# The second expert's first product by seven products of quarters, with the sums of x and of its weights made during the first expert

## The chip, the cores and the metric

One core of a Trainium2 chip runs the whole program. TensorE (PE) multiplies, VectorE (DVE), ScalarE (ACT) and GpSimd (POOL) work on tiles in SBUF and PSUM, and SyncE (SP) issues most DMAs. The metric is the device time of one execution in microseconds, the median of several runs; lower is better.

## The reference

A causal attention with a forgetting bias (2 batches, 8 heads, 576 positions, head size 64) gives 1152 tokens of 512 numbers. A layer of 8 experts and a bilinear layer follow, all in float32:

```python
logits = x @ w_gate; P = np.exp(logits - logits.max())
for _ in range(8):
    P /= P.sum(1, keepdims=True) + 1e-09
    P /= P.sum(0, keepdims=True) + 1e-09
    P *= N / E
for e in range(E):
    h = np.maximum(x @ w1[e], 0.0)      # 1152 x 1024
    out += P[:, e:e + 1] * (h @ w2[e])
...
return (x2 @ w_a) * (x2 @ w_b) @ w_out
```

Every expert sees all tokens.

## The kernel before

Each float32 operand is held as two float16 parts, high and low, and each product is three matmuls (high by high, high by low, low by high). `x` stands transposed in `xt`, two parts of four chunks of 128 rows by 1152 tokens, written tile by tile (9 tiles of 128 tokens) as the attention ends. The first expert (number 0) has plain products per tile, put in between the attention's work as filling for PE.

An expert's first product (`x @ w1[e]`, relu) has two forms. `h_plain` (line 1298, used for expert 1 alone) takes three blocks of 384 tokens and eight rows of outputs, 12 matmuls of 384 columns each (`h_item`, lines 1005 to 1007). ScalarE writes the high part of the relu and DVE the low part (lines 1010 and 1011). `h_seven` (experts 2 to 7) splits `x` by features and tokens, and the weights by features and outputs, into quarters and takes seven products instead of eight (lines 1400 to 1402, 288 columns each). It needs four sums of quarters of `x` (tile `sx`, made once by `x_sums`, lines 1324 and 1328) and four sums of quarters of the weights (`w_sums`, lines 1358, 358 and 372, for each expert), and adds PSUM results on ScalarE and DVE (lines 1415 and 1419). `slot` says in which unit of float16 weights each of the seven quarters or sums stands. The second product (`h @ w2[e]`, lines 1048 to 1050) runs tile by tile into two PSUM banks, which DVE adds into `acc`, scaled by the gate's weight (line 1458).

The weights of an expert come by DMA into two staging tiles, ScalarE sums squares (line 355, or 548 where `fine`), the greatest is found over the partitions (by PE where `early`, lines 520 to 522, else by GpSimd, line 509), and from the scale ScalarE writes the high parts (line 358) and DVE the low parts (line 372). With `fine`, GpSimd may take a share of both (lines 362, 366 and 367). The eight rounds of the gate's normalisation (`sinkhorn`, lines 1151 to 1187) run on DVE with a small matmul in each (line 1175).

All work is put into a graph with costs and ranks, and a planner writes out the order of each engine. Operations ahead of `g.cut` are ranked again: four times, the planner goes backwards from the end of PE's work and gives each operation its latest start as its rank. Those behind the cut keep their ranks and are placed after, so on each engine they stand behind all that is ahead of the cut. `switch` gives back the attention's buffers when all tiles of `xt` are written, and takes the buffers of the experts (`ht`, `sx`, `jk`, the units 4 to 6, `mr`, `ts`) in their place; nothing can be written into those before. Before the change, the weights of expert 1 are prepared ahead of the cut, and `x_sums` runs with rank 202.5 behind it, during expert 1.

Of the kernel before, what the change touches and what calls it, by code (L numbers as in the profile page):

```python
# [10 lines left out]
F32 = mybir.dt.float32  # L11
F16 = mybir.dt.float16
# [234 lines left out]
def forgetting_attention_moe_bilinear_kernel(  # L247
# [14 lines left out]
    nc = tc.nc  # L262
    B, H, S, D = q.shape
# [6 lines left out]
    KF = FF // 128  # L270
# [3 lines left out]
    NB = NTL // BT  # L274
    BN = BT * 128
# [8 lines left out]
    g = Graph()  # L284
# [18 lines left out]
    stage = [const.tile([128, 2048], F32, name=f"stage{i}") for i in range(2)]  # L303
    units = [const.tile([128, 2, 4, 512], F16, name=f"wun{i}") for i in range(4)]
# [3 lines left out]
    HT = NT // 2  # L308
    CN = HT // 2
# [101 lines left out]
    st = [aps.tile([128, 512], F32, name=f"st{i}") for i in range(NST)]  # L411
# [12 lines left out]
    def mbk(m):  # L424
# [11 lines left out]
          w=["clamp"], rank=0)  # L436
# [4 lines left out]
    for b in range(B):  # L441
        sl = slice(b * S, (b + 1) * S)
        g.add("DVE", 1335, lambda sl=sl: nc.vector.tensor_tensor_scan(
            out=ncum[:, sl], data0=one_b, data1=sn[:, sl], initial=0.0, op0=ALU.mult, op1=ALU.add),
# [522 lines left out]
    def frank():  # L967
        fr[0] += 1
        return 1e4 + fr[0]
# [133 lines left out]
    def switch():  # L1103
        att.close()
        bp = ctx.enter_context(tc.tile_pool(name="big", bufs=1))
        for i in range(4, 7):
            units.append(bp.tile([128, 2, 4, 512], F16, name=f"wun{i}"))
        big["ht"] = bp.tile([128, 2, KF, NT], F16, name="ht")
        big["sx"] = bp.tile([128, 4, 2, 2, HT], F16, name="sx")
        big["jk"] = bp.tile([128, 1024], F16, name="jk")  # L1110
        big["mr"] = bp.tile([128, 2048], F32, name="mr")
        for i in range(2):
            big["ts", i] = bp.tile([128, 1024], F32, name=f"ts{i}")
            big["s5", i] = bp.tile([128, CN], F32, name=f"s5_{i}")
            big["w", i] = bp.tile([128, CN], F32, name=f"w22_{i}")
            big["o", i] = big["ts", i][:, 0:DM]
        stage.append(big["mr"])
        for i in range(2):
            units.append(stage[i].bitcast(F16).rearrange("p (z c f) -> p z c f", z=2, c=4))
        big["g0"] = big["sx"].rearrange("p i z c t -> p (i z c t)").rearrange("p (z f t) -> p z f t", z=2, f=4)  # L1120
        yp = ctx.enter_context(tc.tile_pool(name="ps_y", bufs=1, space=PSUM))
        mb.append(yp.tile([128, 512], F32, name="mb2"))
        for i in range(5):
            yb.append(yp.tile([128, 512], F32, name=f"yb{i}"))
# [4 lines left out]
    def hk(z, f, c0=0, c1=NT):  # L1129
        return [("h", z, f, i) for i in range(c0 // 32, (c1 + 31) // 32)]  # L1130

    allh = [x for z in range(2) for f in range(KF) for x in hk(z, f)]
    sxk = [("sx", i, z, c) for i in range(4) for z in range(2) for c in range(2)]
    bigk = ([("u", i, z, c) for i in range(4, 7) for z in range(2) for c in range(4)] + [("yb", i) for i in range(5)] + allh + sxk
            + [("o", i) for i in range(2)] + [("a", i) for i in range(2)] + [("s5", i) for i in range(2)] + [("w", i) for i in range(2)]
            + [("st", 2, c) for c in range(4)] + mbk(2) + ["switch"])
    g.add("-", 0, switch, r=attk, w=bigk)
# [157 lines left out]
    def h_cols(c0, c1):  # L1295
        return (lambda z, f: big["ht"][:, z, f, c0:c1]), (lambda z, f: hk(z, f, c0, c1))

    def h_plain(e):

        for b in range(NB):  # L1300
            dst, dkey = h_cols(b * BN, (b + 1) * BN)
            for f in range(KF):
                h_item(e, b * BN, BN, f, dst, dkey)

    def slot(i):
        return (0, 1, 4, 5)[i // 2], 2 * (i % 2)

    def slot_keys(i):
        u, c0 = slot(i)
        return [("u", u, z, c) for z in range(2) for c in (c0, c0 + 1)]  # L1310

    quad = lambda z, r, t: xt[:, z, 2 * r:2 * r + 2, t * HT:(t + 1) * HT]

    def x_sums():

        rk = 202.5
        sk, uk = [("o", 0), ("a", 0)], [("o", 1), ("a", 1)]
        xk = [("xt", t) for t in range(NTL)]
        for c in range(2):
            S, U = (lambda: big["ts", 0][:, 0:HT]), (lambda: big["ts", 1][:, 0:HT])  # L1320
            q = lambda z, r, t, c=c: quad(z, r, t)[:, c]

            def tt(out, a, b, op, r, w):
                g.add("DVE", 750, lambda: nc.vector.tensor_tensor(out=out(), in0=a(), in1=b(), op=op), r=r, w=w, rank=rk)

            def split(i, src, keys, c=c):
                hi, lo = (lambda: big["sx"][:, i, 0, c]), (lambda: big["sx"][:, i, 1, c])
                g.add("ACT", 700, lambda: nc.scalar.activation(hi(), src(), AF.Copy), r=keys, w=[("sx", i, 0, c)], rank=rk)
                tt(lo, src, hi, ALU.subtract, keys + [("sx", i, 0, c)], [("sx", i, 1, c)])

            X = lambda z, r, t, q=q: (lambda: q(z, r, t))
            add, sub = ALU.add, ALU.subtract
            tt(S, X(0, 0, 1), X(0, 1, 1), add, xk, sk)
            tt(U, X(1, 0, 1), X(1, 1, 1), add, xk, uk)
            tt(S, S, U, add, uk, sk)
            split(0, S, sk)
            tt(U, X(0, 0, 0), X(1, 0, 0), add, xk, uk)
            tt(S, S, U, sub, uk, sk)
            split(1, S, sk)
            tt(U, X(0, 1, 0), X(1, 1, 0), add, xk, uk)  # L1340
            tt(U, U, S, sub, sk, uk)
            split(3, U, uk)
            tt(S, X(0, 0, 0), X(0, 0, 1), sub, xk, sk)
            tt(U, X(1, 0, 0), X(1, 0, 1), sub, xk, uk)
            tt(S, S, U, add, uk, sk)
            split(2, S, sk)

    def w_sums(e, rank):

        z0, z1 = wst[1, e]  # L1350
        sx = ws[1, e]
        half = lambda z, r: (lambda: stage[z][:, r * 1024:(r + 1) * 1024])
        hkeys = lambda z, r: [("st", z, 2 * r), ("st", z, 2 * r + 1)]
        T = [(lambda i=i: big["ts", i]) for i in range(2)]
        tk = [[("o", i), ("a", i)] for i in range(2)]

        def sub(out, a, b, r, w):
            g.add("DVE", 1280, lambda: nc.vector.tensor_tensor(out=out(), in0=a(), in1=b(), op=ALU.subtract), r=r, w=w, rank=rank)

        def split(i, src, keys):  # L1360
            u, c0 = slot(i)
            part = [lambda y=y: units[u][:, y, c0:c0 + 2].rearrange("p c f -> p (c f)") for y in range(2)]
            k = [[("u", u, y, c) for c in (c0, c0 + 1)] for y in range(2)]
            g.add("ACT", 1144, lambda: hi_of(part[0](), src(), sx), r=keys + [("ws", 1, e)], w=k[0], rank=rank)
            g.add("DVE", 1290, lambda: lo_of(nc.vector, part[1](), src(), sx, part[0]()), r=keys + [("ws", 1, e)] + k[0], w=k[1], rank=rank)

        b11, b21, b12, b22 = half(z0, 0), half(z0, 1), half(z1, 0), half(z1, 1)
        k11, k21, k12, k22 = hkeys(z0, 0), hkeys(z0, 1), hkeys(z1, 0), hkeys(z1, 1)
        sub(T[0], b12, b11, k12 + k11, tk[0])
        sub(T[1], b22, b12, k22 + k12, tk[1])  # L1370
        split(3, T[0], tk[0])
        split(4, T[1], tk[1])
        sub(T[0], b22, T[0], k22, tk[0])
        split(5, T[0], tk[0])
        sub(T[0], b21, T[0], k21, tk[0])
        split(6, T[0], tk[0])
        split(0, b11, k11)
        split(1, b21, k21)
        split(2, b22, k22)

    def h_seven(e):
# [7 lines left out]

        def prod(i, j, c, bank, bk, first):  # L1390
            src, keys, wi = ops[i]
            u, ch0 = slot(wi)

            def mm():
                p = bank()[:, 0:CN]
                wt = units[u]
                for ch in range(2):
                    wh, wl = (wt[:, z, ch0 + ch, j * 128:(j + 1) * 128] for z in range(2))
                    xh, xl = (src(z, ch, c * CN) for z in range(2))
                    nc.tensor.matmul(p, lhsT=wh, rhs=xh, start=first and ch == 0, stop=False, skip_group_check=True)  # L1400
                    nc.tensor.matmul(p, lhsT=wh, rhs=xl, start=False, stop=False, skip_group_check=True)  # L1401
                    nc.tensor.matmul(p, lhsT=wl, rhs=xh, start=False, stop=ch == 1, skip_group_check=True)  # L1402

            g.add("PE", 6 * (CN / 2.4 + 2.7), mm, r=keys + slot_keys(wi), w=bk, rank=frank())

        def out(src, bk, f, s_, c):
            c0 = s_ * HT + c * CN
# [279 lines left out]
                    m2_prep(wi, pc, 6, prank())  # L1687
                m2_out(wi, x, prank())

    w_prep(1, 1, (4, 5), 150, fine=True, rel=REL_E1)()  # L1690
    g.cut = len(g.ops)
    early[0] = False
    dense[0] = True
    sinkhorn()
    g.add("PE", 700, set_bits, r=[("xt", t) for t in range(NTL)], w=[("yb", i) for i in range(2, 5)], rank=frank())
    for e in range(1, E):
        last = e == E - 1
        if e == 1:
            h_plain(e)
        else:  # L1700
            h_seven(e)
        w_prep(2, e, (2, 3), prank())()
        if e == 1:
            x_sums()
        if not last:
            w_prep(1, e + 1, (None, None), prank())
        g.add("-", 0, lambda: None, r=hk(0, 0), w=["hold"])
# [78 lines left out]
```

## Time and profile before

| | us |
|---|---|
| median of 3 runs | 1061.39 (1060.77 to 1062.57) |
| the profiled execution | 1059.17 |
| its span, first to last instruction | 1057.3 |
| PE busy | 1008.0 |
| DVE busy | 720.3 |
| ACT busy | 517.4 |
| POOL busy | 156.2 |

The span lies inside the execution's time. Busy times are sums over the whole span; the kernel runs through stages (attention with the first expert to about 231 us, seven more experts, then the bilinear layer), so a share of the span says little of a single stage. The granted clock of PE is the full 2.4 GHz in nearly all of it (0.995 in the mean).

### The profile page before, as it was taken

Reading aid. Unit: us, or ns where it says so; the run is one execution under the profiler, and the core shown is the slowest. Engines: PE = TensorE matmul, PEld = TensorE weight load, DVE = VectorE, ACT = ScalarE, POOL = GpSimd, SP = SyncE. Lnnn points to the kernel's source line nnn. Section 1 sums busy time; section 2 is a strip of 40 time slices with the busy share of each in tenths; the row PEclk is TensorE's granted clock in tenths of the full one; section 3 lists DMA queues with packets and bytes.
Section 4 is the critical chain, followed back from the end, with each engine's and each line's share of the span. In section 5 each row is a group of like instructions: output and inputs, shape, how many; then the busy total and the mean of one; then the engine's idle time right before and its main releaser. Section 6 shows DMA issues by size and latency. Waiting matters only on the chain.

```text
span 1057.3 us, 18899 instructions
## 1 busy us (share of the span) xinstructions
PE 1008.0 (95%) x7676; PEld 625.6 (59%) x7676; DVE 720.3 (68%) x1488; ACT 517.4 (49%) x970; POOL 156.2 (15%) x190
## 2 busy tenths in 40 slices
PE   1688999999999999999999999999999999999998
PEld 0577777866546745754774674575476464555445
DVE  7986865159975898795789889489768684434201
ACT  5786567346535635653672774455355354343100
POOL 4876755320000000000000000000000000000000
PEclk9989999999999999999999999999999999999999
DMA  9883751021123134423324340431443652300001
GB/s 243 166 201 80 163 79 25 2 75 56 41 80 120 41 122 158 160 81 120 120 81 153 131 155 40 158 122 40 160 160 144 184 121 80 127 34 1 20 31 40
DMA packets 123063, 108.75 MB, mean 103 GB/s; under 512 B 87632, under 2 KB 100176, under 8 KB 119136
## 3 DMA queue, kind: packets, MB, share of 16 engines
q1 hardware_dynamic: 121632, 106.74, 33.9%
q8 instruction: 60, 0.98, 0.4%
q10 hardware_dynamic: 1344, 0.81, 0.3%
q14 instruction: 27, 0.22, 0.1%
HBM read 75.29 MB, written 18.09 MB: 88 GB/s over the span
## 4 chain that ended last, share of the span: by engine, by line
PE 88%; DVE 6%; SPq 2%; DMA 1%; issue 1%; ACT 1%; POOL 1%; DVEq 0%; POOLq 0%; ACTq 0%
PE yb L1048 10%; PE yb L1049 10%; PE yb L1050 10%; PE yb L1400 4%; PE yb L1402 4%; PE yb L1401 4%; PE mb L1400 3%; PE mb L1402 3%; PE mb L1401 3%; PE yb L1656 2%; PE yb L1654 2%; PE yb L1655 2%; PE yb L1584 2%; PE yb L1586 2%; PE yb L1585 2%; PE mb L1584 1%
## 5 line engine op out<-in xcount | busy, mean ns | idle before, releaser
L1048 PE MATMUL yb<-wun,ht 128*128 128x512 f16 x504 | 191.0, 379 | 0.0
L1050 PE MATMUL yb<-wun,ht 128*128 128x512 f16 x504 | 191.0, 379 | 0.0
L1049 PE MATMUL yb<-wun,ht 128*128 128x512 f16 x504 | 191.0, 379 | 0.0
L372 DVE SCALAR_TENSOR_TENSOR wun<-stage,sc,wun 128x1024 f16<-128x1024 f32 (+1 forms) x65 | 78.9, 1236 | 11.6 <-ACT wun L358 11.5
L1050 PEld LDWEIGHTS <-ht 128*128 128x128 f16 x504 | 49.3, 98 | 59.5
L1400 PE MATMUL yb<-sx,wun 128*128 128x288 f16 x288 | 82.3, 286 | 2.0 <-DVE sc L343 1.1
L1458 DVE SCALAR_TENSOR_TENSOR acc<-yb,pe,acc 128x512 f32<-128x512 f32 x63 | 47.3, 750 | 53.7 <-PE yb L1050 52.7
L1049 PEld LDWEIGHTS <-ht 128*128 128x128 f16 x504 | 49.3, 98 | 57.7 <-issue 0.3
L1048 PEld LDWEIGHTS <-ht 128*128 128x128 f16 x504 | 49.3, 98 | 57.6
L1402 PE MATMUL yb<-sx,wun 128*128 128x288 f16 x288 | 82.4, 286 | 0.0
L1401 PE MATMUL yb<-sx,wun 128*128 128x288 f16 x288 | 82.3, 286 | 0.0
L1401 PEld LDWEIGHTS <-wun 128*128 128x128 f16 x672 | 65.7, 98 | 22.3 <-issue 4.0
L1400 PEld LDWEIGHTS <-wun 128*128 128x128 f16 x672 | 65.7, 98 | 18.4
L1402 PEld LDWEIGHTS <-wun 128*128 128x128 f16 x672 | 65.7, 98 | 16.6
L358 ACT ACTIVATE wun<-stage,sc 128x1024 f16<-128x1024 f32 (+1 forms) x60 | 60.9, 1040 | 28.3 <-PE yb L1050 14.0
L355 ACT ACTIVATE jk<-stage 128x1024 f16<-128x1024 f32 x52 | 54.7, 1052 | 35.8 <-DMA stage<-in_moe_w_dram 35.3
L904 POOL TENSOR_TENSOR pt<-p,pt 128x512 f16<-128x512 f32 (+1 forms) x48 | 57.1, 1192 | 31.7 <-ACT pt L901 22.6
L1410 ACT ACTIVATE ht<-yb 128x288 f16<-128x288 f32 x96 | 38.8, 406 | 40.7 <-PE yb L1402 40.1
L1400 PE MATMUL mb<-xt,wun 128*128 128x288 f16 x192 | 54.9, 286 | 0.0
L1401 PE MATMUL mb<-xt,wun 128*128 128x288 f16 x192 | 54.9, 286 | 0.0
L1402 PE MATMUL mb<-xt,wun 128*128 128x288 f16 x192 | 54.9, 286 | 0.0
L1411 DVE SCALAR_TENSOR_TENSOR ht<-yb,ht 128x288 f16<-128x288 f32 x96 | 43.0, 453 | 17.1 <-ACT ht L1410 16.7
(358 smaller groups left out, 2639.3 us busy)
## 6 DMA issues: line engine op xcount, KB each, us to landing
stage<-in_moe_w_dram SPq DMA_DIRECT2D x26, 1024.0 KB, 5.3
md<-wun SPq DMA_DIRECT2D x15, 1024.0 KB, 3.9
wun<-md SPq DMA_DIRECT2D x11, 1024.0 KB, 5.0
mr<-in_moe_w_a_dram SPq DMA_DIRECT2D x12, 512.0 KB, 5.8
mr<-in_moe_w_b_dram SPq DMA_DIRECT2D x12, 512.0 KB, 3.9
mr<-in_moe_w_out_dram SPq DMA_DIRECT2D x6, 1024.0 KB, 4.9
stage<-in_moe_w_dram SPq DMA_DIRECT2D x22, 256.0 KB, 4.0
stage<-md SPq DMA_DIRECT2D x4, 1024.0 KB, 4.8
```

The source lines that it names most:

```text
L355: nc.scalar.activation(out, src, AF.Square, accum_out=dst)
L358: nc.scalar.activation(hi, src, AF.Copy, scale=scale)
L372: eng.scalar_tensor_tensor(out=lo, in0=src, scalar=scale, in1=hi, op0=ALU.mult, op1=ALU.subtract)
L904: lambda hi=hi, lo=lo, src=src: nc.gpsimd.tensor_tensor(out=lo, in0=src, in1=hi, op=ALU.subtract)),
L1048: nc.tensor.matmul(pp, lhsT=hh, rhs=wh, start=(f == 0), stop=False)
L1049: nc.tensor.matmul(pp, lhsT=hh, rhs=wl, start=False, stop=False)
L1050: nc.tensor.matmul(pp, lhsT=hl, rhs=wh, start=False, stop=(f == KF - 1))
L1400: nc.tensor.matmul(p, lhsT=wh, rhs=xh, start=first and ch == 0, stop=False, skip_group_check=True)
L1401: nc.tensor.matmul(p, lhsT=wh, rhs=xl, start=False, stop=False, skip_group_check=True)
L1402: nc.tensor.matmul(p, lhsT=wl, rhs=xh, start=False, stop=ch == 1, skip_group_check=True)
L1411: g.add("DVE", 160 + 1.04 * CN, lambda: nc.vector.scalar_tensor_tensor(out=hl(), in0=src(), scalar=0.0, in1=hh(), op0=ALU.max, op1=ALU.sub ...
L1458: g.add("DVE", 663, lambda t=t, z=z: nc.vector.scalar_tensor_tensor(out=acc[:, t], in0=yb[z], scalar=pe[:, t, e:e + 1], in1=acc[:, t], op0 ...
```

## The change

Expert 1 takes `h_seven` as the later experts do. Its seven quarters and sums of weights go into the units 4, 5, 6 and 9 (9 is the tile `mr` seen as a unit), since the units 0 to 3 hold the first expert's weights. `x_sums` and `w_sums(1)` are moved ahead of the cut and so are ranked backwards from its end. Of `x_sums`, one half (`c == 0`) stays on DVE and the other goes to GpSimd, with its own scratch in rows of `ht`. The weights of expert 1 are no longer prepared `fine`, and their maximum is taken by GpSimd.

```diff
--- before.py
+++ after.py
@@ -1117,6 +1117,7 @@
         stage.append(big["mr"])
         for i in range(2):
             units.append(stage[i].bitcast(F16).rearrange("p (z c f) -> p z c f", z=2, c=4))
+        units.append(stage[2].bitcast(F16).rearrange("p (z c f) -> p z c f", z=2, c=4))
         big["g0"] = big["sx"].rearrange("p i z c t -> p (i z c t)").rearrange("p (z f t) -> p z f t", z=2, f=4)
         yp = ctx.enter_context(tc.tile_pool(name="ps_y", bufs=1, space=PSUM))
         mb.append(yp.tile([128, 512], F32, name="mb2"))
@@ -1131,7 +1132,7 @@
 
     allh = [x for z in range(2) for f in range(KF) for x in hk(z, f)]
     sxk = [("sx", i, z, c) for i in range(4) for z in range(2) for c in range(2)]
-    bigk = ([("u", i, z, c) for i in range(4, 7) for z in range(2) for c in range(4)] + [("yb", i) for i in range(5)] + allh + sxk
+    bigk = ([("u", i, z, c) for i in (4, 5, 6, 9) for z in range(2) for c in range(4)] + [("yb", i) for i in range(5)] + allh + sxk
             + [("o", i) for i in range(2)] + [("a", i) for i in range(2)] + [("s5", i) for i in range(2)] + [("w", i) for i in range(2)]
             + [("st", 2, c) for c in range(4)] + mbk(2) + ["switch"])
     g.add("-", 0, switch, r=attk, w=bigk)
@@ -1295,35 +1296,34 @@
     def h_cols(c0, c1):
         return (lambda z, f: big["ht"][:, z, f, c0:c1]), (lambda z, f: hk(z, f, c0, c1))
 
-    def h_plain(e):
-
-        for b in range(NB):
-            dst, dkey = h_cols(b * BN, (b + 1) * BN)
-            for f in range(KF):
-                h_item(e, b * BN, BN, f, dst, dkey)
-
-    def slot(i):
-        return (0, 1, 4, 5)[i // 2], 2 * (i % 2)
-
-    def slot_keys(i):
-        u, c0 = slot(i)
+    def slot(e, i):
+        return ((0, 1, 4, 5) if e > 1 else (4, 5, 6, 9))[i // 2], 2 * (i % 2)
+
+    def slot_keys(e, i):
+        u, c0 = slot(e, i)
         return [("u", u, z, c) for z in range(2) for c in (c0, c0 + 1)]
 
     quad = lambda z, r, t: xt[:, z, 2 * r:2 * r + 2, t * HT:(t + 1) * HT]
 
-    def x_sums():
-
-        rk = 202.5
-        sk, uk = [("o", 0), ("a", 0)], [("o", 1), ("a", 1)]
+    def x_sums(rk):
+
         xk = [("xt", t) for t in range(NTL)]
         for c in range(2):
-            S, U = (lambda: big["ts", 0][:, 0:HT]), (lambda: big["ts", 1][:, 0:HT])
+            if c == 0:
+                eng, cost = "DVE", 750
+                S, U = ((lambda i=i: big["ts", i][:, 0:HT]) for i in range(2))
+                sk, uk = ([("o", i), ("a", i)] for i in range(2))
+            else:
+                eng, cost = "POOL", 1350
+                S, U = ((lambda f=f: big["ht"][:, 0, f].bitcast(F32)) for f in (3, 7))
+                sk, uk = (hk(0, f) for f in (3, 7))
             q = lambda z, r, t, c=c: quad(z, r, t)[:, c]
 
-            def tt(out, a, b, op, r, w):
-                g.add("DVE", 750, lambda: nc.vector.tensor_tensor(out=out(), in0=a(), in1=b(), op=op), r=r, w=w, rank=rk)
-
-            def split(i, src, keys, c=c):
+            def tt(out, a, b, op, r, w, eng=eng, cost=cost):
+                e = nc.vector if eng == "DVE" else nc.gpsimd
+                g.add(eng, cost, lambda: e.tensor_tensor(out=out(), in0=a(), in1=b(), op=op), r=r, w=w, rank=rk)
+
+            def split(i, src, keys, c=c, tt=tt):
                 hi, lo = (lambda: big["sx"][:, i, 0, c]), (lambda: big["sx"][:, i, 1, c])
                 g.add("ACT", 700, lambda: nc.scalar.activation(hi(), src(), AF.Copy), r=keys, w=[("sx", i, 0, c)], rank=rk)
                 tt(lo, src, hi, ALU.subtract, keys + [("sx", i, 0, c)], [("sx", i, 1, c)])
@@ -1358,7 +1358,7 @@
             g.add("DVE", 1280, lambda: nc.vector.tensor_tensor(out=out(), in0=a(), in1=b(), op=ALU.subtract), r=r, w=w, rank=rank)
 
         def split(i, src, keys):
-            u, c0 = slot(i)
+            u, c0 = slot(e, i)
             part = [lambda y=y: units[u][:, y, c0:c0 + 2].rearrange("p c f -> p (c f)") for y in range(2)]
             k = [[("u", u, y, c) for c in (c0, c0 + 1)] for y in range(2)]
             g.add("ACT", 1144, lambda: hi_of(part[0](), src(), sx), r=keys + [("ws", 1, e)], w=k[0], rank=rank)
@@ -1389,7 +1389,7 @@
 
         def prod(i, j, c, bank, bk, first):
             src, keys, wi = ops[i]
-            u, ch0 = slot(wi)
+            u, ch0 = slot(e, wi)
 
             def mm():
                 p = bank()[:, 0:CN]
@@ -1401,7 +1401,7 @@
                     nc.tensor.matmul(p, lhsT=wh, rhs=xl, start=False, stop=False, skip_group_check=True)
                     nc.tensor.matmul(p, lhsT=wl, rhs=xh, start=False, stop=ch == 1, skip_group_check=True)
 
-            g.add("PE", 6 * (CN / 2.4 + 2.7), mm, r=keys + slot_keys(wi), w=bk, rank=frank())
+            g.add("PE", 6 * (CN / 2.4 + 2.7), mm, r=keys + slot_keys(e, wi), w=bk, rank=frank())
 
         def out(src, bk, f, s_, c):
             c0 = s_ * HT + c * CN
@@ -1687,21 +1687,20 @@
                     m2_prep(wi, pc, 6, prank())
                 m2_out(wi, x, prank())
 
-    w_prep(1, 1, (4, 5), 150, fine=True, rel=REL_E1)()
+    early[0] = False
+    w_prep(1, 1, (None, None), 150, rel=REL_E1)
+    x_sums(202.0)
+    w_sums(1, 203.0)
     g.cut = len(g.ops)
-    early[0] = False
     dense[0] = True
     sinkhorn()
     g.add("PE", 700, set_bits, r=[("xt", t) for t in range(NTL)], w=[("yb", i) for i in range(2, 5)], rank=frank())
     for e in range(1, E):
         last = e == E - 1
+        h_seven(e)
         if e == 1:
-            h_plain(e)
-        else:
-            h_seven(e)
+            g.add("-", 0, lambda: None, w=[("u", 9, z, c) for z in range(2) for c in range(4)] + [("st", 2, c) for c in range(4)])
         w_prep(2, e, (2, 3), prank())()
-        if e == 1:
-            x_sums()
         if not last:
             w_prep(1, e + 1, (None, None), prank())
         g.add("-", 0, lambda: None, r=hk(0, 0), w=["hold"])
```

## Rows read from the trace of the kernel before

**Rows 1.** The page's first part: busy us (share of the span) and instructions.

```profile
PE 1008.0 (95%) x7676; PEld 625.6 (59%) x7676; DVE 720.3 (68%) x1488; ACT 517.4 (49%) x970; POOL 156.2 (15%) x190
```

**Rows 2.** Windows: us, then busy us (instructions) of each engine, PEclk, DMA share, GB/s.

```profile
200.00:208.00 8.00, 8.00 (x91) 4.77 (x89) 1.65 (x6) 1.19 (x2) 0.00 (x0) 1.00 0.01 2
...
231.00:281.45 50.45, 49.36 (x310) 30.27 (x308) 48.30 (x135) 27.57 (x51) 3.75 (x4) 1.00 0.24 84
...
430.00:460.00 30.00, 28.44 (x219) 21.18 (x218) 24.29 (x59) 19.11 (x44) 1.50 (x2) 1.00 0.40 136
```

**Rows 3.** PE timeline: start us, us, instructions [idle before]; second expert's products.

```profile
231.59 0.33 PE L1005 MATMUL mb<-xt,wun 128*128 128x384 f16 x1
...
231.75 0.33 PE L1006 MATMUL mb<-xt,wun 128*128 128x384 f16 x1
...
234.69 0.27 PE L520 MATMUL yb<-id,sc 128*1 128x128 f32 x1 [0.99 <-DVE sc L1151]
...
281.45 0.38 PE L1048 MATMUL yb<-wun,ht 128*128 128x512 f16 x1
...
292.18 0.38 PE L1048 MATMUL yb<-wun,ht 128*128 128x512 f16 x1
```

**Rows 4.** DVE timeline: start and end of the normalisation's chain.

```profile
234.42 0.21 DVE L1151 TENSOR_REDUCE sc<-logit 128x1 f32<-128x72 f32 x1
...
291.38 1.55 DVE L1458 SCALAR_TENSOR_TENSOR acc<-yb,pe,acc 128x512 f32<-128x512 f32 x2
```

**Rows 5.** PE timeline, third expert: two matmuls of 288 columns, ten places apart.

```profile
328.44 0.29 PE L1400 MATMUL mb<-sx,wun 128*128 128x288 f16 x1
...
329.66 0.29 PE L1401 MATMUL mb<-xt,wun 128*128 128x288 f16 x1
```

**Rows 6.** DVE groups by form: shapes, count | busy us, mean ns | idle.

```profile
L1324 DVE TENSOR_TENSOR ts<-xt 128x576 f32<-128x576 f16 x12 | 8.9, 750 | 0.1
...
L1358 DVE TENSOR_TENSOR ts<-stage 128x1024 f32<-128x1024 f32 x6 | 7.3, 1217 | 0.0
...
L372 DVE SCALAR_TENSOR_TENSOR wun<-ts,sc,wun 128x1024 f16<-128x1024 f32 x24 | 30.7, 1278 | 0.2 <-ACT wun L358 0.2
```

**Rows 7.** GpSimd (POOL) timeline.

```profile
17.13 0.69 POOL L362 TENSOR_SCALAR qa<-acc,cst 128x512 f16<-128x512 f32 x1
...
18.57 1.15 POOL L367 TENSOR_TENSOR kn<-acc,kn 128x512 f16<-128x512 f32 x1
...
226.58 4.06 POOL L362 TENSOR_SCALAR wun<-stage,sc 128x512 f16<-128x512 f32 x4 [16.07 <-DVE sc L343]
...
231.82 1.47 POOL L367 TENSOR_TENSOR wun<-stage,wun 128x512 f16<-128x512 f32 x1
```

**Rows 8.** DVE and ACT timelines: the attention's end, the first work in new buffers.

```profile
207.78 0.16 DVE L936 TENSOR_SCALAR rs<-xp 128x4 f32<-128x4 f32 x1 [5.27 <-PE xp L924]
...
214.04 0.62 ACT L548 ACTIVATE wun<-stage 128x512 f16<-128x512 f32 x1
```

**Rows 9.** DVE timeline beside GpSimd's operations.

```profile
18.61 1.66 DVE L372 SCALAR_TENSOR_TENSOR qb<-acc,cst,qa 128x512 f16<-128x512 f32 x1
...
227.19 7.31 DVE L372 SCALAR_TENSOR_TENSOR wun<-stage,sc,wun 128x512 f16<-128x512 f32 x7 [0.85 <-ACT wun L358]
...
232.20 1.64 DVE L372 SCALAR_TENSOR_TENSOR wun<-stage,sc,wun 128x512 f16<-128x512 f32 x1
```

**Rows 10.** Line 372: count: ns min/median/max, first and last start us, forms.

```profile
L372 DVE SCALAR_TENSOR_TENSOR qb<-acc,cst,qa x3: 743/744/1660, 18.6 to 52.0; 128x512 f16<-128x512 f32 x3
```

**Rows 11.** PE timeline: two neighbouring rounds of the normalisation.

```profile
241.23 0.34 PE L1175 MATMUL yb<-pe,ones 128*128 128x72 f32 x2
...
247.25 0.34 PE L1175 MATMUL yb<-pe,ones 128*128 128x72 f32 x2
```

**Rows 12.** Windows, as in 2: an idle PE and the clock after it.

```profile
65.00:68.00 3.00, 1.43 (x30) 1.05 (x29) 2.93 (x6) 2.27 (x4) 2.70 (x3) 1.00 0.78 102
...
71.00:74.00 3.00, 3.00 (x36) 3.00 (x34) 2.47 (x2) 2.98 (x6) 2.92 (x4) 0.50 0.07 14
```

## The prediction

> **What bounds the kernel now.** I read the page's first part first: TensorE is busy for 95% of the span, so a change counts where it takes columns from PE or makes PE wait [rows 1]. Then I read the busy time by stage, because the share over the span hides where another engine sets the pace. In the first product of the second expert (231 to 281.45 us) PE is busy for 49.36 of 50.45 us and DVE for 48.30: two engines are full at once, and GpSimd is nearly empty [rows 2]. Third came the timelines of that stretch. The first product begins at 231.59, the second at 281.45, and the third output tile of the second product begins at 292.18 instead of right after two tiles [rows 3]. It waited for DVE: there are two banks for these tiles, and the first is emptied by the accumulation that DVE starts at 291.38, at the end of a chain that began at 234.42 with the maximum of the gate's logits and went through eight rounds of row and column sums [rows 4]. So two things bound this stretch: PE's columns, and a chain of DVE and PE that is 57 us long. The end of the kernel moves with the start of that third tile, since PE is full behind it; I call this start M. Before, M is 292.18.
>
> **What PE gains.** The plain product takes 288 matmuls of 384 columns, 0.16 us from one to the next (231.59 to 231.75); by the longer count of [rows 11], where 36 of them and a small one fill 6.02 us, it is 0.1625, 46.8 us. Seven products of quarters take 336 matmuls of 288 columns at 0.122 us (ten from 328.44 to 329.66, the same form in the third expert) [rows 3, 5], 41.0 us: 5.8 us less. With 1.4 us for the eight small matmuls of the normalisation and some 0.6 us of waits, and without the 1.0 us wait at 234.69 [rows 3], a product that could start at 231 would end at 274.0 and M, two tiles or 10.5 us later, would be 284.5: a gain of 7.7 us. That is the best case.
>
> **What must be done before the product can start.** The plain product needs only two units of the expert's weights as they are. The seven products need the sums of x (all tiles of it) and seven quarters or sums of weights, and the order of the products asks for all seven within the first 6 to 8 us. On DVE this is 14 operations on half of x at 0.75 us (10.5), four differences of weights at 1.22 (4.9) and seven low parts at 1.28 (9.0) [rows 6]: 24.4 us by durations, which overlap a little from one to the next, so it is an upper count. GpSimd has the other 14 on x. The nearest row is a TENSOR_TENSOR of 512 columns at 1.15 us [rows 7]; for 576 that is 1.29, and 18.1 us in all. None of it can start before the last tile of x is transposed and the attention's buffers are given back. I call that moment T. In the trace it is 214, where ScalarE begins to square the second expert's weights, the first work in the new buffers [rows 8]. What goes away is small: seven low parts on DVE that ended at 234.4, and six operations on GpSimd [rows 7, 9].
>
> **Whether DVE and GpSimd work side by side.** This decides the sum. At 18.57 GpSimd starts a TENSOR_TENSOR and takes 1.15 us [rows 7]; at 18.61 DVE starts an operation with two SBUF inputs, which takes 1.66 us, against 0.743 for the fastest of its group [rows 9, 10]. It ends 0.55 us behind GpSimd's end: nearly its whole work came after. At 231.82 a DVE operation is under way first: GpSimd's takes 1.47 us, 0.32 more, and the DVE operation that starts at 232.20 takes 1.64 and again ends 0.55 us behind it [rows 7, 9]. All of the sums on DVE, of x and of the weights, have two inputs in SBUF. So they take turns with GpSimd. The other bound is the stretch from 226.58 to 234.42: seven DVE operations (0.743 alone, 5.2 us) and six of GpSimd (five of 0.69 and one of 1.15 alone, 4.6 us; the fifth isn't among the rows) took 7.84 us for 9.8 us of work [rows 7, 9, 10], a factor of 0.80. By that factor the 24.4 and 18.1 us take 34.0; by turns without any overlap 42.5; side by side 24.4. DVE also has some relus of the first expert, which read PSUM, and waits for ScalarE's high parts; they can lie in GpSimd's turns. I take 37.5 us after T, near the middle of the two measured bounds (38.2), and 27 as the far end, side by side with 3 us of other work.
>
> The Trainium skill (SBUF — State Buffer, "Who interferes with whom") states that a DVE instruction with two SBUF inputs contends with a GpSimd instruction that reads SBUF, and that the loser is fully blocked, not slowed. The rows of this trace agree: the DVE operation ends 0.55 us behind GpSimd's in both places. By the rule alone the port's work would end 42.5 us after T, which would put M 5 us later than the forecast has it; without it, 27 us.
>
> **Where T goes.** The sums now belong to the part that is ranked backwards from its end, and their ranks pull the last attention tile forward. DVE's costs in the code (14 of 750, four of 1280, seven of 1290) come to 24.7 us, so the planner wants T some 27 us before the end of the first expert, near 204. It can have this: from 200 to 208 ScalarE is busy for 1.19 of 8 us and GpSimd not at all, while PE is full with the first expert's tiles [rows 2], and the last attention product is read at 207.78 [rows 8]. I take T = 204; unmoved it is 214. The planner does not know that the engines take turns, so the port's work ends at D = 204 + 37.5 = 241.5, where it expects 231.
>
> **What follows for M.** On PE: the relus of the last tiles queue on DVE behind the sums, so the first expert ends close to D, and I let the product start at D - 1 = 240.5, run 41.0 + 1.4 + 0.6 us to 283.5 and be followed by two tiles (10.5 us): M = 294.0. On DVE: the chain of the normalisation is queued behind the sums, as it is planned after them. Before, it took 57 us [rows 4], of which eight rounds of 6.02 us (PE 241.23 to 247.25) [rows 11]; a round waits for a free place between PE's groups of 1.95 us (12 matmuls), and the new groups are 0.74 us, so I take 5.2 to 5.3 us a round, 51 us in all: M = 241.5 + 51 + 0.8 = 293.3. The later one, 294.0 (D + 52.5), is 1.8 us after the old M. To this comes what an idle PE does to its clock: at 65 to 68 us PE was busy for 1.43 of 3 us, and at 71 to 74 the granted clock was 0.50, the lower of its two levels, 1.2 GHz [rows 12]. A PE that runs from slot to slot before D may lose up to 3 us so; I take 0.7. DVE's load in the product is near full (48 relu parts and sums, and the normalisation), but the 20 us of x's sums are gone from it. A stretch of the fourth expert's first product with DVE at 24.29 of 30 us cost PE 1.56 us [rows 2]; the 0.6 above is my share of such waits, 2 the upper bound.
>
> SP's queue: the weights of the second expert now leave their staging buffers only when the sums are done, near D; the next load is 5 us, and the low parts follow some 15 us later, 25 us before the second product needs them. I cost this at nothing; the cover is the 41 us of the product. GpSimd's maximum over partitions is queued behind up to two of its own sums, about 3 us, which the sums of x cover. Unit 9 and GpSimd's scratch cost nothing: the tile `mr` is first loaded during the third expert, and the scratch rows of `ht` are among the last that the product writes.
>
> **The sum.** M moves by +2.5 us. The profiled execution is 1059.17 us (span 1057.3 and 1.9 around it), 2.2 under the median. With the shift it is 1061.7, and the median 1061.4 becomes 1063.9.
>
> **The rivals.** First, faster: the port's work ends by 236, because T moves to about 200 or because the engines overlap more than the two places show. The stretch from 200 to 208 speaks for an early T [rows 2], [rows 7, 9] against the overlap. M is then 236 + 52.5 = 288.5 (the later of the two paths), and the kernel 3.7 us faster, 1058; at most 7.7, 1054. This decides as soon as D is below 237.5.
>
> Second, much slower: T stays near 214, as other work of the last attention tile holds it. D is 251.5 and M 304.0, 12 us later: 1073. For it speaks that T is bound to a chain of four engines, against it that PE alone was full there. With T half way it is 1068.
>
> Third, nothing: D is near 239.5, and what PE saves in the product is exactly waited for again at the third tile, as the chain of the normalisation only starts at D. M is 292.0, the time 1061. That is also what one would see if the sums were not hidden by the first expert but only moved ahead of the product.
>
> **How the numbers follow.** Forecast 0.45 (own range 1061.5 to 1067.5, a third of it within 0.2%, about 2.1 us, which is what a measurement can tell from no change), faster rival 0.25, much slower 0.15, nothing 0.15. Faster: 0.24 + 0.03 from the edge of the third. Same: 0.15 + 0.12 + 0.01. Slower: 0.30 + 0.15. The range reaches from 5.9 us under to 9.6 over the old median and leaves out the best end of the first rival and the worst of the second.
>
> **What would show it.** T, the start of the first sum of x on DVE: 204 right, over 210 the second rival. Turns at the port are right if GpSimd's sums take 1.7 us in the mean and DVE's among them 1.5 to 2; 1.3 and 0.75 would make them wrong. The first matmul of the seven products near 240 with idle time ahead of it put down to DVE; M near 294.5. A first product that starts by 233 makes the prediction wrong, whatever its cause.

## The result and the profile after

The changed kernel takes 1071.62 us (median of 4 runs, 1069.17 to 1072.19), the kernel before 1061.3 beside it: a ratio of 1.0091, with a 95% interval of 1.0073 to 1.0109. It is slower, as the forecast had it, but by 10 us and not by 2.5: the time lies at the upper end of the range, 1071.0 (0.6 us past it by the median, at it by the ratio), and not near the forecast. The profiled execution took 1072.19 us, its span is 1070.4, which is 13.1 us over the span of before.

The page's first part (to be read against [rows 1]) shows that the saving is real: PE is busy 6.6 us less, with 45 matmuls more.

```profile
PE 1001.4 (94%) x7721; PEld 626.4 (59%) x7721; DVE 736.5 (69%) x1506; ACT 524.2 (49%) x986; POOL 169.9 (16%) x196
```

PE's timeline, against [rows 3]: the product starts at 246.67, where the plain one started at 231.59, and the third output tile of the second product (M) at 302.87 instead of 292.18. From the start of the product to M it is 56.2 us, 4.4 less than the 60.6 of before. So the product is shorter, and it starts 15 us later.

```profile
224.20 0.58 PE L1048 MATMUL mb<-wun,h 128*128 128x512 f16 x1 [10.00 <-DVE sc L339]
...
246.67 0.30 PE L1400 MATMUL mb<-sx,wun 128*128 128x288 f16 x1
...
302.87 0.38 PE L1048 MATMUL yb<-wun,ht 128*128 128x512 f16 x1
```

DVE's timeline has T, the first sum of x, at 198.17, and D, where the last low part ends and the normalisation begins (L1152 is line 1151 of before), at 245.10. The sums take 46.9 us from T.

```profile
198.17 2.51 DVE L1324 TENSOR_TENSOR ts<-xt 128x576 f32<-128x576 f16 x2 [1.38 <-DMA xt<-xhl]
...
223.46 0.69 DVE L1035 SCALAR_TENSOR_TENSOR h<-mb,h 128x512 f16<-128x512 f32 x1 [9.57 <-ACT h L1034]
...
243.90 1.28 DVE L372 SCALAR_TENSOR_TENSOR mr<-ts,sc,mr 128x1024 f16<-128x1024 f32 x1 [0.61 <-ACT mr L358]
245.10 0.22 DVE L1152 TENSOR_REDUCE sc<-logit 128x1 f32<-128x72 f32 x1
```

The windows (columns as in [rows 2]) hold a stretch that nothing in the prediction had: from 214 to 224 PE works for 0.20 us, DVE for 0.54 and ScalarE for 2.23. After it PE runs at a mean granted clock of 0.67 for 7 us, which by itself costs 2.3 us.

```profile
214.00:224.00 10.00, 0.20 (x4) 0.13 (x2) 0.54 (x1) 2.23 (x4) 4.93 (x4) 0.72 0.00 0
224.00:231.00 7.00, 6.80 (x22) 2.65 (x22) 6.36 (x9) 4.83 (x5) 6.84 (x5) 0.67 0.00 0
```

GpSimd's timeline tells why. Between its fourth and its fifth sum lies the maximum over the partitions (L509), with 5.97 us of idle time ahead of it and 7.14 behind it. The label "DVE ts L1324" of the first isn't the cause: the operand of the maximum, from line 502 on DVE, was there at 206.9, 4.5 us before. Nor do DVE's sums keep a maximum out: in the second of the three versions below it starts beside them 0.14 us after its operand (203.77 against 203.63), with 10 us of idle time ahead of it. "issue" means that the engine waited for nothing that the profile shows.

```profile
203.76 1.67 POOL L1324 TENSOR_TENSOR ht<-xt 128x576 f32<-128x576 f16 x1
211.40 0.38 POOL L509 PARTITION_ALL_REDUCE sc<-sc  x1 [5.97 <-DVE ts L1324]
218.92 1.26 POOL L1324 TENSOR_TENSOR sx<-ht,sx 128x576 f16<-128x576 f32 x1 [7.14 <-issue]
```

The view of the single lines shows what lies in those gaps: on GpSimd's queue (POOLq) an instruction MODIFY_POOL_CONFIG, under line 509 first at 205.6 and under line 1324 at 211.7. From 205.6 to 211.40 it is 5.8 us, from 211.8 to 218.92 it is 7.1. In the kernel before, this stands under line 509 at 233.5 only, with 12 us of idle time behind it: the next maximum came at 245.27. What the engine does in such a gap, no trace here shows.

```profile
L509 POOLq MODIFY_POOL_CONFIG  x4: 7/8/8, 205.6 to 237.6; - x4
...
L1324 POOLq MODIFY_POOL_CONFIG  x2: 83/83/83, 211.7 to 211.8; - x2
```

The Trainium skill (GPSIMD Engine Reference, "2.1 Instruction dispatch") states that the first call of a freshly loaded GpSimd function costs some 6 us more, with no instruction in the profile to show for it. The first gap agrees roughly (5.8 us from the instruction to the maximum); the second is the way back to the ordinary sums, and costs more.

How the gap reaches the other engines is read on ScalarE: its order has the high part of a sum that GpSimd makes ahead of the first expert's relus. It waits 12.06 us for that sum, the relus stand behind it, DVE's low parts behind them (the 9.57 above), and PE behind those (the 10.00).

```profile
221.69 0.68 ACT L1328 ACTIVATE sx<-ht 128x576 f16<-128x576 f32 x1 [12.06 <-POOL ht L1324]
222.28 0.67 ACT L1328 ACTIVATE sx<-ts 128x576 f16<-128x576 f32 x1
222.85 1.06 ACT L1034 ACTIVATE h<-mb 128x512 f16<-128x512 f32 x2
```

### The profile page after: what moved, and what is told of

It is laid out like the page before. It is cut to its first block, busy times and chain, and to the rows that moved or that the text cites. A ratio compares the mean times of both kernels' runs of the same rounds, so it can differ in the third digit from the quotient of the medians.

```text
span 1070.4 us, 19039 instructions
## 1 busy us (share of the span) xinstructions
PE 1001.4 (94%) x7721; PEld 626.4 (59%) x7721; DVE 736.5 (69%) x1506; ACT 524.2 (49%) x986; POOL 169.9 (16%) x196
## 4 chain that ended last, share of the span: by engine, by line
PE 81%; DVE 11%; issue 3%; DMA 2%; POOL 2%; ACT 1%; POOLq 0%; DVEq 0%; SPq 0%; ACTq 0%
PE yb L1049 10%; PE yb L1050 10%; PE yb L1048 10%; PE yb L1400 4%; PE yb L1402 4%; PE yb L1401 4%; PE mb L1400 3%; PE mb L1401 3%; PE mb L1402 3%; DVE wun L372 2%; PE yb L1654 2%; PE yb L1655 2%; PE yb L1656 2%; PE yb L1584 2%; PE yb L1585 2%
## 5 line engine op out<-in xcount | busy, mean ns | idle before, releaser
L1400 PE MATMUL yb<-sx,wun 128*128 128x288 f16 x336 | 96.1, 286 | 2.2 <-DVE sc L343 1.1
L1402 PE MATMUL yb<-sx,wun 128*128 128x288 f16 x336 | 96.1, 286 | 0.0
L1401 PE MATMUL yb<-sx,wun 128*128 128x288 f16 x336 | 96.1, 286 | 0.0
L1401 PEld LDWEIGHTS <-wun 128*128 128x128 f16 x768 | 75.1, 98 | 28.9 <-issue 8.1
L1400 PEld LDWEIGHTS <-wun 128*128 128x128 f16 x768 | 75.5, 98 | 20.6
L1402 PEld LDWEIGHTS <-wun 128*128 128x128 f16 x768 | 75.1, 98 | 18.9
L355 ACT ACTIVATE jk<-stage 128x1024 f16<-128x1024 f32 x56 | 59.0, 1053 | 42.5 <-DMA stage<-in_moe_w_dram 40.8
L1410 ACT ACTIVATE ht<-yb 128x288 f16<-128x288 f32 x112 | 45.3, 406 | 46.2 <-PE yb L1402 45.5
L1400 PE MATMUL mb<-xt,wun 128*128 128x288 f16 x224 | 64.1, 286 | 0.8 <-ACT yb L1419 0.8
L1402 PE MATMUL mb<-xt,wun 128*128 128x288 f16 x224 | 64.1, 286 | 0.0
L1401 PE MATMUL mb<-xt,wun 128*128 128x288 f16 x224 | 64.1, 286 | 0.0
L1411 DVE SCALAR_TENSOR_TENSOR ht<-yb,ht 128x288 f16<-128x288 f32 x112 | 50.1, 453 | 17.0 <-ACT ht L1410 16.5
L509 POOL PARTITION_ALL_REDUCE sc<-sc x14 | 10.3, 738 | 308.6 <-DVE sc L502 302.7
```

The lines of the kernel that those rows point to most:

```text
L355: nc.scalar.activation(out, src, AF.Square, accum_out=dst)
L1410: g.add("ACT", 52 + 120 + CN / 1.2, lambda: nc.scalar.activation(hh(), src(), AF.Relu), r=bk, w=k0, rank=-5)
L1411: g.add("DVE", 160 + 1.04 * CN, lambda: nc.vector.scalar_tensor_tensor(out=hl(), in0=src(), scalar=0.0, in1=hh(), op0=ALU.max, op1=ALU.sub ...
```

## The experiments

T and D below are read as above. Theory A: the changes of GpSimd's configuration make the loss. Theory B: DVE and GpSimd take turns, and the gap only moves the waiting.

**The maximum alone, put into the kernel before.** Line 509 takes the maximum for the second expert's first weights, everything else is as before:

```diff
+    early[0] = False
     w_prep(1, 1, (4, 5), 150, fine=True, rel=REL_E1)()
     g.cut = len(g.ops)
-    early[0] = False
```

> The kernel before (plain product, two units of weights prepared in fine pieces, which GpSimd shares), with one part of the change alone: the maximum on GpSimd instead of PE. Theory A: some 6 us before the maximum are hidden by the squares, but some 7 us behind it GpSimd can't begin its part of the high and low parts; the last low part ends near 238 to 240 instead of 234.4, the kernel is 2 to 5 us slower, 1063 to 1066. Rival (changing costs nothing, the stall came from the turns): the two PE steps and their waits go, 1060 to 1061.5.

Measured: 1067.14 us, ratio 1.0058 [1.0039, 1.0077]. GpSimd's timeline:

```profile
219.89 0.38 POOL L509 PARTITION_ALL_REDUCE sc<-sc  x1 [8.56 <-DVE sc L502]
227.62 3.12 POOL L362 TENSOR_SCALAR wun<-stage,sc 128x512 f16<-128x512 f32 x4 [7.35 <-issue]
```

and behind it DVE's low parts, and PE:

```profile
229.01 2.27 DVE L372 SCALAR_TENSOR_TENSOR wun<-stage,sc,wun 128x512 f16<-128x512 f32 x2 [6.45 <-POOL wun L362]
...
231.94 0.59 PE L1048 MATMUL mb<-wun,h 128*128 128x512 f16 x1 [7.06 <-DVE h L1035]
```

The way to the maximum is hidden here, by the wait for its operand; the way back takes 7.35 us, DVE waits 6.45 us for the high parts behind it, PE waits 7.06 us for a relu that stands behind DVE's low parts, and the kernel is 6 us slower. It needs no sum of x: one maximum among GpSimd's ordinary operations is enough. The price was above what I expected, and came by another way: the last low part ends at 235.1 (before 234.4) and not at 238 to 240, and the loss is PE's wait for the first expert.

**The changed kernel without the maximum.** GpSimd copies each partition's own value at the same place, with the same cost, so the order of all engines stays (`own` is set for this one maximum only, by lines that aren't shown):

```diff
-            g.add("POOL", 1200, lambda: nc.gpsimd.partition_all_reduce(a, m, 128, RMAX), r=[mk], w=ak, rank=rank)
+            only = own[0]
+            g.add("POOL", 1200, lambda: nc.gpsimd.tensor_copy(a, m) if only else nc.gpsimd.partition_all_reduce(a, m, 128, RMAX), r=[mk], w=ak, rank=rank)
```

> The changed kernel with one edit: the maximum over the partitions of the second expert's first weights is left out; in its place GpSimd copies each partition's own value, at the same place in its order and with the same cost in the graph. So GpSimd has nothing of another kind to do between two of its sums. Theory A (the two changes of GpSimd's configuration, 5.8 and 7.1 us, stop x's sums, and through ScalarE's order everything else): T stays near 198, the 10 us stretch near 214 to 224 in which all engines stand still is gone, the last low part of the weights ends at 234 to 237 instead of 245, and the time is 8 to 12 us under the changed kernel's, 1059 to 1063. Theory B (the sums are late because DVE and GpSimd take turns; the gap only moves the waiting): the last low part ends no earlier than 242 and the time is 1067 or more.

**The same, with GpSimd's sums replaced by fills.**

```diff
-                g.add(eng, cost, lambda: e.tensor_tensor(out=out(), in0=a(), in1=b(), op=op), r=r, w=w, rank=rk)
+                g.add(eng, cost, lambda: e.tensor_tensor(out=out(), in0=a(), in1=b(), op=op) if eng == "DVE" else e.memset(out(), 0.0), r=r, w=w, rank=rk)
```

> As the run f1_copy, and GpSimd's 14 sums of x are replaced by 14 fills of the same outputs, which read nothing (half of x's sums and the maximum over the partitions are left out). DVE's work and the planner's order are the same. If the two engines take turns where both have inputs in SBUF (A): DVE's sums go back from 1.2 to 1.8 us to 0.75 and 1.25, the last low part ends 27 to 31 us after T, at 226 to 231, and the time is 2 to 7 us under that of f1_copy; not more, since the first expert itself ends at 231. If turns cost nothing (B): the same T, the same end of the low parts and the same time as f1_copy, within 1.5 us.

Measured: 1063.8 us (ratio 1.0033 [1.0019, 1.0048]) with the copy, 1053.64 (0.9927 [0.9903, 0.9952]) with the fills. The window from T to D with the copy (lines are one higher in these two kernels):

```profile
198.61:239.81 41.20, 32.95 (x363) 22.75 (x361) 40.45 (x39) 21.20 (x31) 25.49 (x15) 0.96 0.11 31
```

In the same stretch three of DVE's groups and GpSimd's first one (shapes, count | busy us, mean ns | idle):

```profile
L1325 DVE TENSOR_TENSOR ts<-xt 128x576 f32<-128x576 f16 x6 | 8.3, 1413 | 1.4 <-DMA xt<-xhl 1.4
L372 DVE SCALAR_TENSOR_TENSOR wun<-stage,sc,wun 128x1024 f16<-128x1024 f32 x3 | 6.9, 2317 | 0.0
...
L1036 DVE SCALAR_TENSOR_TENSOR h<-mb,h 128x512 f16<-128x512 f32 x6 | 4.1, 683 | 0.0
...
L1325 POOL TENSOR_TENSOR ht<-xt 128x576 f32<-128x576 f16 x6 | 10.8, 1800 | 3.5 <-DMA xt<-xhl 3.2
```

The window with the fills:

```profile
197.56:228.12 30.56, 29.93 (x359) 21.95 (x357) 27.63 (x39) 21.32 (x31) 8.16 (x15) 1.00 0.17 42
```

and the same groups there:

```profile
L1325 DVE TENSOR_TENSOR ts<-xt 128x576 f32<-128x576 f16 x6 | 4.4, 752 | 1.4 <-DMA xt<-xhl 1.4
L1036 DVE SCALAR_TENSOR_TENSOR h<-mb,h 128x512 f16<-128x512 f32 x6 | 4.1, 689 | 2.2 <-ACT h L1035 2.2
...
L372 DVE SCALAR_TENSOR_TENSOR wun<-stage,sc,wun 128x1024 f16<-128x1024 f32 x3 | 3.8, 1279 | 0.0
...
L1325 POOL MEMSET ht<- 128x576 f32 x10 | 5.5, 578 | 8.0 <-ACT sx L1329 4.8 <-DMA xt<-xhl 3.2
```

The 10 us gap is gone with the copy, D is 239.8 and not 245.1, and the span is 7.4 us shorter than that of the changed kernel (by the ratios it is 6.2 us, by the medians 7.8). So the maximum with its two gaps is a cause, shown alone. But D did not fall to the 237 that theory A wanted, nor stay past the 242 of theory B, and 1063.8 us lies between their times too: PE still waits 5.2 us in one place there, and the sums fill 41.2 us. The fills show what fills them. The same 39 DVE operations take 40.45 us beside GpSimd's sums and 27.63 beside fills, which read nothing: 12.8 us of DVE's time go to turns with GpSimd. The relus among them (L1036, one input in PSUM) take 0.68 and 0.69 us, so it is the operations with two inputs in SBUF that stretch, not all of DVE. The fills are also shorter than the sums (8.16 us of GpSimd against 25.49), so that the two runs differ in this as well; but DVE is busy for 40.45 of the 41.20 us with the copy, so it is DVE's time that sets D there. D comes 41.2 us after T with the sums and 30.6 with the fills, and the span falls by another 11.1 us. Both theories are right, each for a part, and I had the turns' price too low: 2 to 7 us were expected of this run.

**Who makes the sums, who finds the maximum.** Three versions of the changed kernel: the maximum by PE, half of x's sums on GpSimd as in the change; the maximum on GpSimd, all sums on DVE; the maximum by PE and all sums on DVE. The two edits are

```diff
+    w_prep(1, 1, (None, None), 150, rel=REL_E1)
     early[0] = False
-    w_prep(1, 1, (None, None), 150, rel=REL_E1)
     x_sums(202.0)
```
```diff
-            if c == 0:
+            if c < 2:
```

> The changed kernel, with the maximum over partitions of the second expert's weights taken by PE as before, so that GpSimd has nothing but sums of x in this stretch. Theory A (the 10 us in which all engines stood still at 214 to 224 is GpSimd changing between the maximum and elementwise work, and ScalarE, DVE and PE queue behind it): no gap on GpSimd, the sums begin near 198 and the last low part of the weights ends near 235 to 236 instead of 245; 9 to 13 us faster than the changed kernel, 1058 to 1063. Theory B (the sums are late because DVE and GpSimd take turns at a port, and the gap is a side effect): the last low part stays past 242, 1068 or more.

> The changed kernel with both halves of x's sums on DVE; GpSimd takes only the maximum. Theory A: GpSimd changes once, after its last work for the attention, while nothing needs it, so there is no gap; DVE needs 24.4 + 10.5 us and some relus, 38 us in all, which the planner knows and so asks for the attention's end still earlier: last low part at 231 to 234, 1054 to 1059. Rival (the maximum on GpSimd is slow in itself): 5 us or more between the weights' last square and the scale, 1062 or more. If DVE and GpSimd worked side by side, this kernel would have to be 8 to 10 us slower than e1_pe_max; if they take turns, it is the same or up to 4 us faster.

> Both at once: maximum by PE and all of x's sums on DVE; GpSimd does nothing here. Theory A with turns at the port: like e2_pool_max_dve within 2 us, 1054 to 1059, and the same as e1_pe_max or up to 4 us faster. Side by side: 8 to 10 us slower than e1_pe_max.

Measured: 1068.07 (ratio 1.0073 [1.0047, 1.0100]), 1061.45 (1.0005 [0.9988, 1.0023]) and 1055.44 (0.9953 [0.9935, 0.9972]). The first result went against theory A, which wanted under 1063: without the maximum on GpSimd there is no gap, but the planner wrote another order, T came 6.5 us later (204.70), D at 246.45, and PE waits for the first expert's low parts (us in total, times, longest):

```profile
PE mb L1048 <- DVE h L1035: 6.4, 2, 5.2
```

So the run doesn't show the maximum's price; the copy above, which keeps the order, does. The second version missed theory A too (1054 to 1059, D at 231 to 234). Both versions with all sums on DVE are faster than the first, by 6.6 and 12.6 us, more than the 4 that I allowed for turns and the opposite of side by side (8 to 10 us slower); and they lie 6 us apart, not within 2. The third version is faster than both kernels, by 0.5% than that of before. Its sums, all on DVE, take 42.2 us from T, as long as with GpSimd's help:

```profile
195.00 1.43 DVE L1324 TENSOR_TENSOR ts<-xt 128x576 f32<-128x576 f16 x2 [2.47 <-DMA xt<-xhl]
...
237.18 0.22 DVE L1152 TENSOR_REDUCE sc<-logit 128x1 f32<-128x72 f32 x1
```

In the second one it is 41.8 us (197.43 to 239.23). So giving GpSimd half of x's sums, 41.2 us with the copy, brought D nearer to T by 1 us at most: DVE is spared 14 operations of 0.75 us, 10.5 us, and loses 12.8 at the port.

**The deadline.** The third version with the cut ahead of the sums, so that they have no deadline:

```diff
     w_prep(1, 1, (None, None), 150, rel=REL_E1)
     early[0] = False
+    g.cut = len(g.ops)
     x_sums(202.0)
     w_sums(1, 203.0)
-    g.cut = len(g.ops)
```

> The version with the maximum by PE and all sums of x on DVE (e3_pe_max_dve, 1055.4), with the sums of x and of the weights put behind the cut: they keep their place in the code but get no deadline. If the early T is what makes the sums fit (A): T goes back to 208 to 214, the sums take the same 42 us from there, the product starts 10 to 17 us later, and the time is 1066 to 1073. If the deadline does not matter (B), as PE's filling is short of work anyway: T and the time stay within 2 us of e3_pe_max_dve.

Measured: 1096.25 us, ratio 1.0333 [1.0302, 1.0363]. The deadline matters, and by far more than I gave it: 41 us against the third version, where I had 11 to 18. The first sum starts at 227.18 and not at 208 to 214, the sums stand between the rounds of the normalisation, and PE, with nothing else to do, falls to the lower clock (windows):

```profile
230.00:240.00 10.00, 3.94 (x16) 2.22 (x16) 9.49 (x28) 4.29 (x7) 0.00 (x0) 0.62 0.00 0
...
260.00:270.00 10.00, 2.27 (x7) 1.26 (x8) 9.55 (x25) 2.96 (x3) 0.00 (x0) 0.50 0.00 0
```

**The planner's costs.** The third version with the costs of DVE's sums raised by 15%, lowered by 10% and raised by 5%; of the first, one of three lines:

```diff
-                eng, cost = "DVE", 750
+                eng, cost = "DVE", 860
```

> e3_pe_max_dve with the planner's costs of DVE's sums of x and of the second expert's weights raised by 15% (750 to 860, 1280 to 1470, 1290 to 1480 ns), and nothing else, so that the planner asks for an earlier T. If each microsecond of T is one of the time (A): T 2 to 5 us earlier than 195 and the time 1051 to 1054. If T can move no further because the last attention tiles are bound by their own chain of four engines (B): T within 1 us of 195 and the time 1054 to 1057.

> As f4_costs, with the planner's costs of the same sums lowered by 10% (675, 1150 and 1160 ns) against e3_pe_max_dve. f4_costs came out 7 us slower than e3_pe_max_dve, where both theories had it faster or the same. If costs under or above the real ones shift T and the time steadily (A): T 2 to 3 us later than 195, the last low part near 240, and the time 1057 to 1060. If a cost changes the written order in ways that have no direction (B, the planner as a throw of the dice): the time lies anywhere between 1053 and 1064, and T need not have moved later.

> As f4_costs, with the costs raised by 5% only (790, 1340 and 1355 ns). A steady dependence (A) puts the time a third of the way from e3_pe_max_dve to f4_costs, 1056 to 1059, with the product's first matmul at 234 to 235. If the order has no direction (B), it lies anywhere between 1053 and 1064. In both, if the stretch around the start of the product decides, the time is 819 to 823 us behind the first matmul of the product, or more only where PE waits inside the product's first groups, as it did in f4_costs.

| costs | T | product starts | span | median |
|---|---|---|---|---|
| 0.90 | 198.5 | 237.13 | 1061.8 | 1060.05 |
| 1.00 | 195.0 | 233.58 | 1053.4 | 1055.44 |
| 1.05 | 198.6 | 241.13 | 1066.3 | 1066.80 |
| 1.15 | 196.5 | 234.93 | 1061.4 | 1062.47 |

(The span is that of the profiled execution.) The time has no direction in the cost: a cost changed by a twentieth moves it by 11 us (10 by the ratios to the kernel before). Both theories of the first of these runs failed, as T did not come earlier and the time rose; of the other two, the second theory holds in that there is no direction, but 1066.8 lies above its range, and the span there ends 825 us behind the product's first matmul, not 819 to 823. What the orders differ by is where the product starts and whether it then runs: with 1.15 it starts early and PE waits 5.3 us in its first groups. So the 1055.44 are the time of one order, a lucky one of four, and the difference of 6 us between the second and the third version above (maximum on GpSimd or by PE) cannot be put down to the maximum; no gap holds up DVE or PE in either. The time of the changed kernel is that of one order as well; only the copy and the fills keep this order, so the prices below rest on these two.

## Why the prediction was right and wrong

**That M sets the end: right.** With the fills the product starts at 230.57, and M is 286.76, 5.4 us earlier than before; the span is 5.4 us shorter. In the changed kernel M is 10.7 us later and the span 13.1 longer; another 2.4 us are lost behind it, most of it in two later experts (PE's waits for the tile `w` of line 1415 there are 2.4 us, before 0.3). With the copy, in the same order, only 0.3 us are lost behind M; no run explained the rest.

**The best case: the term of waits was too small.** I gave the stretch from a product that starts at 231 to M 53.5 us; it is 56.2 with the copy, with the fills and in the changed kernel alike. From the product's start to the end of the tile that is put in at its end PE is idle for 2.34 of 51 us, where I had 0.6 (the other 1 us of the 2.7 isn't traced):

```profile
246.70:297.70 51.00, 48.66 (x378) 36.83 (x378) 44.49 (x151) 30.46 (x69) 1.62 (x2) 1.00 0.14 46
```

So the gain to be had was 5.4 us of span, not 7.7.

**T: too late in the sum.** I had 204, it was 198.2; all the versions with a deadline lie between 195 and 204.7. A likely reason, not tried: the planner counts DVE's relus with the sums (30.6 us, as the fills show, and the first expert ends at 231), and I counted the sums alone. The second rival (T stays at 214) is excluded.

**The port: the value in the middle was wrong.** Of the bounds 24.4, 34.0 and 42.5 I took 37.5. Without the gap it is 41.2 (the copy). GpSimd's sums take 1.78 us in the mean (24.9 us for 14), as forecast for turns, and DVE's L1324 group 1.41 instead of 0.75. The Trainium skill (SBUF — State Buffer, "Who interferes with whom") was the better guide: by its rule alone the work would end after 42.5 us. That only reads of GpSimd lock the port agrees too, as the fills leave DVE at 0.752. The factor of 0.80 came from a stretch of other operations (five of GpSimd's six there were TENSOR_SCALARs, [rows 7]) and did not carry over to these; why it was milder wasn't tried. The far end, 27, was too low also: with the fills it is 30.6, of which DVE is busy for 27.6 and idle for 2.9, most of this in waits for ScalarE's high parts of the relus (2.2), which I had at nothing.

**GpSimd's maximum: the step that failed.** I wrote that it is queued behind up to two sums, "about 3 us, which the sums of x cover". What it costs is not the queue but the two changes of configuration, 5.8 and 7.1 us, and nothing covers them, because ScalarE's order binds the first expert to GpSimd's sums. D moved from T + 41.2 to T + 46.9 by it, M by 5.3 us, and the span by 7.4. The instruction stood in the trace of before, at 233.5, ahead of idle time.

**Errors that hid each other.** The kernel without the maximum has the median that I forecast, 1063.8 us. That isn't merit. Its M is 297.58, where I had 294.0: T was earlier (-5.4 us), the port's work longer (+3.7), the product began 1.6 us after D and not 1 before it (+2.6), and from there to M it took longer (+2.7), together +3.6. The ledger reads, on M: -5.4 for the seven products, +10.8 for GpSimd's sums in place of fills, +5.3 for the maximum, together +10.7; with the 2.4 behind M, whose cause is open, the span's +13.1. So the direction came out by the cause that I gave, the turns, while half of the move on M is a term that I had at nothing. The two prices go by the order in which the causes are taken out: in the changed kernel, where the gap keeps the engines apart, DVE's 39 operations take 35.45 us in the 46.93 from T to D, so the turns stretch them by 7.8 there and not by 12.8, and the gap hides the rest.

**The chain of the normalisation: not the bound, as said, and shorter.** A round takes 4.59 us (I had 5.2 to 5.3, and [rows 11] 6.02), as the groups of PE that it waits for are shorter:

```profile
249.62 0.34 PE L1176 MATMUL yb<-pe,ones 128*128 128x72 f32 x2
...
254.21 0.34 PE L1176 MATMUL yb<-pe,ones 128*128 128x72 f32 x2
```

**The clock** cost up to 2.3 us (0.67 over 7 us) and not 0.7, behind a gap that I didn't have; with the fills it is 1.00 from T to D. SP's queue cost PE nothing that the trace shows.

## What to carry to other kernels

Before work is given to GpSimd, look in the trace for what it does between: a change from its ordinary operations to a maximum over partitions and back took 13 us of its time here and 5.3 us of M, with nothing in the busy times to show for it; where the engine was idle anyway, it cost nothing. For operations with two inputs in SBUF, GpSimd was no second engine beside DVE: with 14 of 28 sums moved to it the work ended 1 us earlier at most. And where a planner writes the order, change its costs by a few per cent before a few microseconds are put down to a design.

## What was unexpected of the hardware

The change of GpSimd's configuration took 5.8 us on the way to the maximum over the partitions and 7.1 and 7.35 us on the way back to elementwise operations, in three gaps of two kernels. The maximum itself is 0.38 us there. And the loss by turns was larger on DVE than the work moved away from it (10.5 us): 12.8 us for 14 sums of GpSimd, 0.92 us each.
